# A Fourier mixing layer and a tanh-shrink MLP on one core: one third of batch 1's first stage in the prologue, half of batch 0's first matrix made on chip, other places for copies and loads

## The chip, the cores and the metric

The kernel runs on one core of a Trainium2 chip. A core has a matrix engine (PE, which loads its stationary operand in a step of its own, PEld), a vector engine (DVE), an activation engine (ACT), a general engine (POOL) and a queue engine (SP), which work at the same time and wait for each other by semaphores. Transfers between DRAM and on-chip memory run on 16 DMA engines; SP, ACT and POOL issue them, each on a queue of its own. An engine takes its instructions strictly in the order in which the program gives them, so a transfer that has to wait holds up all that its engine would do next. The metric is the device time of one execution in microseconds (us); less is better.

## The reference

```python
x = randn(8, 3008, 256) * 0.1          # batch, sequence, channels
X = rfft(x, axis=1)                    # 1505 frequencies
Y = X * (filt_r + 1j * filt_i)
y = irfft(Y, n=3008, axis=1)           # as float32
x = y.reshape(24064, 256)
h = x @ w_in                           # 256 x 2048, float64 on input
g = h - tanh(h)
out = g @ w_out                        # 2048 x 256, float64 on input
```

The outputs are 24064 x 256 float32 numbers.

## The kernel before

**The transform in four stages.** The sequence of 3008 is split as 64 x 47. With the symmetry n and 47-n, 24 residues r are left (`NH`). `first` multiplies, for each r, the 128 rows of x (64 rows for r, 64 for 47-r) by a 128 x 128 matrix `f` of cosines and sines; its 128 output rows are four blocks of 32 frequencies (`NA`): cosine and sine for each of two combinations. The result goes to DRAM (`ct1`). `middle` takes seven groups (`SLOTS`) of up to five frequencies each: `forth` mixes the 24 residues (matrices in `mats`), `filtered` multiplies by the filter, and `back` mixes back and writes to DRAM (`ct2`). `last` loads four residues at a time (`load_e2`), and its product with `g` is the input of the MLP. All products are float32.

**The MLP.** There are 48 groups of tokens (8 batches by 6), each with four quarters u of the hidden width: 192 units `U`. In unit U, `up` computes h for quarter U, the activation `shrink` works on U-1 and `down` on U-2. The first units use `up_plain` and `down_plain`, the others a scheme with 7 products in place of 8 (sums of weights, `sums`, and sums of the data, `combine`). The weights come as float64; `converted` turns a part (`raw`, 512 KB) into float32 by one ACT and six or seven DVE instructions. The eight parts of w_in are converted in the prologue, those of w_out (`late`) around its end.

**What sets the order.** The program records instructions by hand (`manual_schedule`): the order in the source is the order on each engine. Generators are stepped with `next`. In the main loop each unit has five points t(0) to t(4); the point's number in a batch is pos = 20c+5u+k, with c the group in the batch and u the quarter. `planned` spreads the 12 steps of `first` for a batch two ahead, and the 58 of `middle` for the next one, evenly over these points; while batch 0 is worked on, the steps of `first` for batch 2 have the points 2 to 34 (`LEAD`) and `middle` of batch 1 the points 34 to 104 (`LAG`). At a point, at most one due step is taken. A step of `first` issues the loads of the step two ahead (`begin`: `f` and two or three pieces of x, all by SP), two matmuls of 128 x 256, an ACT copy and a write by ACT.

**The prologue.** It does batch 0's `first` (`first0`, three parts of eight residues, with the matrices kept on chip in `f0`), then for the seven groups: `across` (transposes in place of a trip through DRAM), `forth`, `filtered`, and `back0`. Beside it stand the conversion of w_in and, in `first1`, the whole `first` of batch 1 with `f0` (12 steps of two residues; the loads `x1` in three parts, lines 222 to 228; writes at line 991). Tile `filt` has three buffers, filled from the filter inputs for group g+2 while group g is worked on (line 903); `e1`, the staging tile of the writes to `ct2`, has three. The order of transfers in the prologue is fixed by the order of issue on SP, ACT and POOL. For the later batches `filters_d` lays the filters out in DRAM (`filt_d`): it zeroes some rows from a tile `zero` (line 1072), then issues 44 copies from DRAM to DRAM by POOL (line 1081), one at each of t(1) to t(4) from unit 0 on. A function `warmer`, matmuls whose result nobody reads, is defined in the prologue and not called.

**Lines in the profile.** 867: matmuls of `first0`; 870: their copies; 888: transposes of `across`; 282 and 329: matmuls of `forth` and `back`; 298 to 310: `filtered`; 912 and 914: matmuls of `back0`; 917: its copy, 918: its write; 981: matmuls of `first1`; 250: matmuls of `first`; 426: matmuls of `last`; 534, 464: matmuls of `up_plain` and `up`; 688, 634: of `down_plain` and `down`; 141: load of a weight part; 147 to 167: its conversion; 237, 222 to 228: loads of `f` and x; 406, 408: loads for `last`.

Of the kernel before, what the change touches and what calls it, by code (L numbers as in the profile page):

```python
# [9 lines left out]
F32 = mybir.dt.float32  # L10
# [29 lines left out]

TURN, BEND, SCALE = 0.5677082594873644, 0.9282206731669795, 1.0956273529524616
NEAR = 0.6

def _consts():
# [11 lines left out]
    for r in range(NH):  # L56
        for half, n in ((0, r), (1, NR - r)):
# [5 lines left out]
            if r:  # L63
                f[half, :, r, 2, :-1], f[half, :, r, 3, :-1] = -odd * s, odd * c
            plus, minus = (1 + sign(n)) / 2, (1 - sign(n)) / 2
            f[half, :, r, 0, -1], f[half, :, r, 2, -1] = plus, minus
            if r:
                f[half, :, r, 1, -1], f[half, :, r, 3, -1] = odd * plus, odd * minus
# [14 lines left out]
    for k, (a, b) in enumerate(((cos, cos), (cos, -sin), (sin, cos), (-sin, -sin),  # L83
# [4 lines left out]

    return [np.ascontiguousarray(v, dtype=np.float32)
            for v in (f.reshape(128, -1), g.reshape(128, -1), mats, np.eye(128))]  # L90

@with_exitstack
def kernel(
# [11 lines left out]
    f_d, g_d, mats_d, one_d = (nc.inline_tensor(v, name=n).ap()  # L105
                               for v, n in zip(_consts(), ("f", "g", "mats", "one")))
# [125 lines left out]
    def first(b, z):  # L232

        def begin(c):
            w = XH * 128
            f = tr.tile([128, XH, 128], F32, tag="f", bufs=3, name="f")
            nc.sync.dma_start(f, f_d[:, w * c:w * (c + 1)])
            return load_x(tr.tile([128, XH, DM], F32, tag="x", bufs=3, name="x_sb"),
                          b, XH * c, XH), f

        began = {0: begin(0), 1: begin(1)}
        yield
        for c in range(NX):
            if c + 2 < NX:
                began[c + 2] = begin(c + 2)
            xt, f = began.pop(c)
# [27 lines left out]
    def forth(g, at, z):  # L274
# [4 lines left out]
        for v in (1, 0):  # L279
            pa = z("pa", [128, 2, DM])[0:n]  # L280
            for k in range(2):
                nc.tensor.matmul(pa[:, k], way[2 * v + k], at[0:n, 2 * v + k],  # L282
                                 start=True, stop=True)
# [548 lines left out]
    with tc.tile_pool(name="tr", bufs=2) as tr, tc.manual_schedule():  # L832
# [12 lines left out]
        with tc.tile_pool(name="pro", bufs=1) as pro, \  # L845
# [60 lines left out]
            def back0(g, nn):  # L906

                way = ways(g, 1)
                for v in range(2):
# [6 lines left out]
                    e1 = pro.tile([128, 2, DM], F32, tag="e1", bufs=3, name="e1")[0:KM]  # L916
# [11 lines left out]
            jobs = parts_of(range(4))  # L928
            xs, began = [], []
# [19 lines left out]
            G.tensor_copy(gate, xs[1][64:65, 0, 0:1])  # L949
# [6 lines left out]
            early = weights(tiles0, range(4), G, began)  # L956
# [12 lines left out]
            x1s = []  # L969

            def load_x1():

                k = len(x1s)
                x1s.append(load_x(big([128, 8, DM], F32, "x1"), 1, 8 * k, 8))

            def first1():

                for r in range(0, NH, 2):
                    pf = z0("pf", [128, 2, DM])
                    for k in range(2):  # L980
                        nc.tensor.matmul(pf[:, k], f0[:, r + k], x1s[r // 8][:, (r + k) % 8],
                                         start=True, stop=True)
                    pool, tag, bufs = ((pro, "e1", 3) if r < 12 else (tr, "a1", 2) if r < 16
                                       else (tr, "nn", 1) if r < 20 else (tr, "e1", 2))
                    if tag != "nn" or r == 16:
                        a1, n = pool.tile([128, 4 if tag == "nn" else 2, DM], F32, tag=tag,
                                          bufs=bufs, name="a1"), 0
                    ACT.copy(a1[:, n:n + 2], pf)
                    n += 2
                    if n == a1.shape[1]:  # L990
                        (ACT if r < 10 else nc.sync).dma_start(
                            dram(ct1[1], (r + 2 - n) * DM, [[NH * DM, 128], [1, n * DM]]), a1)
                    yield

            ones_1 = first1()
# [21 lines left out]
            for g in range(last_g + 1):  # L1017
# [3 lines left out]
                if g < 3:  # L1021
                    load_x1()
# [15 lines left out]
                if g in (2, 4):  # L1038
                    next(ones_1)
                if g == last_g - 1:  # L1040
# [3 lines left out]
                    fs = first(2, z1)  # L1044
                    next(fs)
            for _ in range(3):
# [3 lines left out]
            for _ in ones_1:  # L1050
                convert(5)
            convert(100)

        with tc.tile_pool(name="dn", bufs=2) as dn, \
# [15 lines left out]
            def filters_d():  # L1070
                zero = tr.tile([128, 2 * DM], F32, tag="a2", bufs=2, name="zero")
# [3 lines left out]
                                                        [1, 2 * DM]]), zero[0:n * SG])  # L1075
                nc.sync.dma_start(dram(filt_d, (n * KM * 4 + 2) * DM, [[4 * DM, 1], [1, 2 * DM]]),
                                  zero[0:1])
                yield
                for g in range(len(SLOTS)):
                    for v, row, n, src in filter_rows(g):  # L1080
                        G.dma_start(dram(filt_d, ((g * KM + row) * 4 + v) * DM,
                                         [[4 * DM, n], [1, DM]]), src)
# [144 lines left out]
```

## Time and profile before

| | |
|---|---|
| median of 3 runs | 2764.23 us |
| lowest, highest | 2760.06, 2765.8 us |
| the profiled execution's own time | 2762.34 us |
| its span, first to last instruction | 2760.5 us |
| PE busy | 2695.6 us |
| DVE, ACT, POOL busy | 1671.0, 1731.5, 1315.9 us |
| mean DMA rate over the span | 75 GB/s |

The profile is of one execution. Busy time counts work, not waiting. Of PE's time two things are not in the busy share: the waits, and how fast it ran, which is the granted clock (PEclk, 1.00 is full). A view by windows gives for each stretch of time the busy time of PE, PEld, DVE, ACT and POOL (in brackets the number of instructions), the granted clock, the mean busy share of the 16 DMA engines and their rate. In the timeline a row is: start, duration of the row's instructions together, engine, line, operation, tiles, count, and in square brackets how long the engine was idle before and what ended it. In the trace a matmul of float32 operands stands as two records (x4 is two matmuls); "SPq" and "ACTq" mark transfers being issued, and their duration is that of the issue.

### The profile page before, as it was taken

How to read it: one execution, taken by the hardware profiler on the slowest of the kernel's cores; microseconds unless marked ns; L12 is line 12 of the kernel's file. 1: busy time of each engine (PE TensorE's matmuls, PEld its weight loads, DVE VectorE, ACT ScalarE, POOL GpSimd, SP SyncE). 2: the span in 40 equal slices, each digit the busy share in tenths (PEclk: the TensorE clock that was granted, in tenths of full speed). 3: DMA queues.
4: the chain of work that ended last, by engine and by line, in shares of the span. 5: the costliest groups of instructions: out<-in, count | busy, mean ns of one | idle time of the engine just before them, and what ended most of it. 6: DMA issues, size and time to landing. Idle time of an engine off the chain costs nothing.

```text
span 2760.5 us, 36254 instructions
## 1 busy us (share of the span) xinstructions
PE 2695.6 (98%) x12866; PEld 2355.3 (85%) x12866; DVE 1671.0 (61%) x2067; ACT 1731.5 (63%) x2595; POOL 1315.9 (48%) x1106
## 2 busy tenths in 40 slices
PE   6899999999999999999999999999999999999998
PEld 5568889888898888988889888898888988899887
DVE  5776766566566665566646665466655766654545
ACT  2466666666666666666666666666666666666665
POOL 3216545454455445544545454445444554454453
PEclk9999999999999999999999999999999999999999
DMA  9743322342233312333124232332322222111010
GB/s 218 247 118 87 83 63 68 78 103 57 63 73 103 89 40 65 89 91 82 48 63 116 66 79 52 85 89 67 83 51 70 53 63 54 30 25 32 21 26 17
DMA packets 334359, 207.50 MB, mean 75 GB/s; under 512 B 226622, under 2 KB 295642, under 8 KB 333785
## 3 DMA queue, kind: packets, MB, share of 16 engines
q1 hardware_dynamic: 291529, 148.31, 23.2%
q10 hardware_dynamic: 38336, 47.72, 5.7%
q0 software_dynamic: 4304, 9.07, 1.3%
q8 instruction: 103, 1.69, 0.3%
q14 instruction: 87, 0.71, 0.1%
HBM read 133.05 MB, written 74.97 MB: 75 GB/s over the span
## 4 chain that ended last, share of the span: by engine, by line
PE 90%; DVE 4%; DMA 3%; issue 2%; ACT 1%; ACTq 0%; POOL 0%; SPq 0%; DVEq 0%; POOLq 0%
PE o L634 38%; PE x L464 22%; PE z L464 11%; PE y L464 5%; PE pa L282 3%; PE pu L426 3%; PE pe L329 3%; PE pf L250 2%; PE o L688 1%; DMA filt<-in_filt_r_dram 1%; DMA ct<-e 1%; DVE h L586 1%; DMA x<-in_x_dram 1%; DVE h L520 1%; DVE h L487 1%
## 5 line engine op out<-in xcount | busy, mean ns | idle before, releaser
L634 PE MATMUL o<-t,wd 128*128 128x256 f32 (+1 forms) x3008 | 760.3, 375 | 0.0
L444 POOL TENSOR_TENSOR t<-h 128x512 f32<-128x512 f32 (+1 forms) x186 | 256.6, 1380 | 922.9 <-DVE h L586 899.7
L586 DVE TENSOR_TENSOR h<-h,y 128x1024 f32<-128x1024 f32 (+1 forms) x384 | 512.8, 1335 | 281.5 <-ACT y L582 280.9
L634 PEld LDWEIGHTS o<-t,wd 128*128 128x128 f32 x3008 | 570.5, 190 | 69.6 <-issue 2.4
L464 PE MATMUL x<-tu,wu 128*128 128x256 f32 (+1 forms) x2256 | 574.0, 377 | 0.5 <-ACT u L470 0.2
L634 PE MATMUL o<-h,wd 128*128 128x256 f32 (+1 forms) x2256 | 571.0, 376 | 1.8 <-DVE h L586 1.8
L464 PEld LDWEIGHTS x<-tu,wu 128*128 128x128 f32 x2256 | 421.9, 190 | 61.6 <-ACT u L470 7.8
L634 PEld LDWEIGHTS o<-h,wd 128*128 128x128 f32 x2256 | 424.2, 190 | 52.7 <-DVE h L586 2.6
L470 ACT COPY s<-x 128x512 f32<-128x512 f32 (+1 forms) x188 | 108.8, 579 | 502.4 <-PE x L464 491.1
L576 ACT ACTIVATE y<-h 128x1024 f32<-128x1024 f32 (+1 forms) x384 | 400.2, 1042 | 12.5 <-ACT a L251 5.6
L579 ACT ACTIVATE y<-y 128x1024 f32<-128x1024 f32 (+1 forms) x384 | 399.6, 1040 | 12.1
L582 ACT ACTIVATE y<-y 128x1024 f32<-128x1024 f32 (+1 forms) x384 | 400.0, 1042 | 4.7
L504 DVE TENSOR_TENSOR h<-z,u 128x512 f32<-128x512 f32 (+1 forms) x188 | 127.5, 678 | 259.1 <-ACT u L470 257.8
L470 ACT COPY u<-x 128x512 f32<-128x512 f32 (+1 forms) x376 | 215.0, 572 | 85.7 <-PE x L464 65.0
L446 POOL TENSOR_TENSOR t<-h 128x512 f32<-128x512 f32 (+1 forms) x186 | 267.0, 1435 | 0.0
L445 POOL TENSOR_TENSOR t<-h,t 128x512 f32<-128x512 f32 (+1 forms) x186 | 259.8, 1397 | 14.6
L447 POOL TENSOR_TENSOR t<-h,t 128x512 f32<-128x512 f32 (+1 forms) x186 | 263.6, 1417 | 0.0
L512 DVE COPY h<-x 128x512 f32<-128x512 f32 (+1 forms) x188 | 127.9, 680 | 157.1 <-PE x L464 156.3
L464 PE MATMUL z<-ut,wu 128*128 128x256 f32 (+1 forms) x752 | 190.3, 375 | 0.0
L464 PE MATMUL z<-tu,wu 128*128 128x256 f32 (+1 forms) x752 | 190.1, 375 | 0.0
L464 PE MATMUL x<-ut,wu 128*128 128x256 f32 (+1 forms) x752 | 190.1, 375 | 0.0
L464 PE MATMUL y<-ut,wu 128*128 128x256 f32 (+1 forms) x752 | 190.0, 375 | 0.0
(137 smaller groups left out, 3085.0 us busy)
## 6 DMA issues: line engine op xcount, KB each, us to landing
e<-ct SPq DMA_DIRECT2D x48, 512.0 KB, 4.3
ct<-e ACTq DMA_DIRECT2D x96, 240.0 KB, 2.5
a<-ct SPq DMA_DIRECT2D x42, 480.0 KB, 6.9
ft<-filt SPq DMA_DIRECT2D x42, 480.0 KB, 7.5
out_dram<-ot SPq DMA_DIRECT2D x1248, 16.0 KB, 1.5
ct<-a ACTq DMA_DIRECT2D x77, 256.0 KB, 3.2
x_sb<-in_x_dram SPq DMA_DIRECT2D x138, 128.0 KB, 4.2
gt<-g SPq DMA_DIRECT2D x48, 256.0 KB, 3.2
```

The source lines that it names most:

```text
L444: by.tensor_sub(t[0], b[0][1], b[0][0])
L445: by.tensor_sub(t[1], b[1][1], t[0])
L446: by.tensor_sub(t[2], b[1][1], b[0][1])
L447: by.tensor_sub(t[3], b[1][0], t[1])
L464: nc.tensor.matmul(bank[:, k], wu[:, q - 1, (2 * u + k) * 128:(2 * u + k + 1) * 128], rhs[q - 1], start=(first and k == 0), stop=True, ski ...
L470: ACT.copy(t, X)
L512: V.tensor_copy(h[:, 2, :, 0:w], X)
L576: ACT.activation(y[k], ht[k], AF.Arctan, scale=TURN)
L579: ACT.activation(y[k], y[k], AF.Tanh, scale=BEND)
L582: ACT.activation(y[k], y[k], AF.Square, scale=SCALE, accum_out=y_sums[:, 2 * U + k // 2:2 * U + k // 2 + 1])
L586: V.tensor_mul(ht[k], ht[k], y[k])
L634: nc.tensor.matmul(product(q), wd[:, q - 1, (2 * u + k) * 128: (2 * u + k + 1) * 128], rhs[q - 1][:, k], start=(u == 0 and k == 0 and q == ...
```

## The change

There are five parts.

1. **Half of the first matrix on chip.** The four blocks of `f` are put in another order (`ORDER`, 0, 2, 3, 1), and `_consts` also returns `f_half`, the first two blocks of each residue. In this order the second half is the first one times +1 or -1, by the half of the partitions (`sgn`), but for two columns that are exchanged. The prologue loads `f_half` by ACT (three transfers of 256 KB in place of 512 KB) into tiles `fh`, and DVE makes `f0` from each with one copy and three multiplications by `sgn`, two of them of a single column per residue. `forth` takes its inputs by `PLACE`.
2. **A third of batch 1's first stage.** `first1` does eight residues (4 steps) in place of 24; one load of `x1`, issued at group 3. The other 8 steps of two residues are put ahead of batch 2's 12 in the generator `first` (`also`), which then has 20 steps at the points 4 to 34, and loads `f` and x for them from DRAM.
3. **Order of the loads at the start.** The first two weight parts are issued ahead of the third part of x, by ACT and SP; the third by POOL ahead of the filters of group 0; the fourth later, since `raw` has three buffers in place of four. `e1` has five in place of three.
4. **Matmuls for the clock.** `warmer` is called four times: 13 times on a tile of ones at the start, 5 and 8 between the parts of `first0`, 10 after the last step of `first1`.
5. **Filter copies by SP.** The 44 copies from DRAM to DRAM are issued by SP in place of POOL, from unit 2 on in place of unit 0; the tile `zero` is taken from `e1`'s buffers in place of `a2`'s.

```diff
+ORDER = (0, 2, 3, 1)
+PLACE = [ORDER.index(j) for j in range(4)]
...
+    f = f[:, :, :, ORDER, :]
     return [np.ascontiguousarray(v, dtype=np.float32)
-            for v in (f.reshape(128, -1), g.reshape(128, -1), mats, np.eye(128))]
+            for v in (f.reshape(128, -1), f[:, :, :, 0:2].reshape(128, -1), g.reshape(128, -1), mats, np.eye(128))]
...
-    def first(b, z):
-
-        def begin(c):
+    def first(b, z, also=()):
+
+        jobs = [*also, *((b, c) for c in range(NX))]
+
+        def begin(k):
+            b, c = jobs[k]
...
-                nc.tensor.matmul(pa[:, k], way[2 * v + k], at[0:n, 2 * v + k],
+                nc.tensor.matmul(pa[:, k], way[2 * v + k], at[0:n, PLACE[2 * v + k]],
...
-            def warmer(n):
-
-                warm = z0("warm", [128, 2, 128])
+            def warmer(n, t=None):
+
+                warm = z0("warm", [128, 256])
+                t = f0[:, 0:2].rearrange("p a n -> p (a n)") if t is None else t
                 for _ in range(n):
-                    nc.tensor.matmul(warm, f0[:, 0], f0[:, 0:2], start=True, stop=True)
+                    nc.tensor.matmul(warm, t[:, 0:128], t, start=True, stop=True)
...
-                    e1 = pro.tile([128, 2, DM], F32, tag="e1", bufs=3, name="e1")[0:KM]
+                    e1 = pro.tile([128, 2, DM], F32, tag="e1", bufs=5, name="e1")[0:KM]
...
-                                bufs={"raw": 4, "top": 2, "low": 1}[k])
+                                bufs={"raw": 3, "top": 2, "low": 1}[k])
...
+                if c == 2:
+                    began += [begun(tiles0, job, queue=q)
+                              for job, q in zip(jobs, (ACT, nc.sync))]
                 nc.sync.dma_start(xt[0:64], dram(x.tensor, r * DM, [[NR * DM, 64], [1, 8 * DM]]))
-                ACT.dma_start(f0[:, r:r + 8], f_d[:, 128 * r:128 * r + 1024])
+                fh = pro.tile([128, 8, 64], F32, tag="e1", bufs=5, name="fh")
+                ACT.dma_start(fh, half_d[:, 64 * r:64 * r + 512])
...
-                if lo:
-                    began += [begun(tiles0, job, queue=q)
-                              for job, q in zip(jobs, (nc.sync, ACT))]
+                V.tensor_copy(f0[:, r:r + 8, 0:64], fh)
+                for to, cols in ((64, slice(0, 64)), (95, slice(63, 64)), (127, slice(31, 32))):
+                    n = cols.stop - cols.start
+                    V.tensor_scalar(out=f0[:, r:r + 8, to:to + n], in0=fh[:, :, cols],
+                                    scalar1=sgn, scalar2=None, op0=ALU.mult)
...
+            began.append(begun(tiles0, jobs[2], queue=G))
             fts = {0: filters_of(0)}
             G.dma_start(mats[:, 3 * KM:], mats_d[:, 3 * KM:])
-            began += [begun(tiles0, job, queue=G) for job in jobs[2:4]]
...
-            convert(7)
+            warmer(13, filt[2][:, 0])
             first0(0)
+            warmer(5)
             convert(7)
             first0(1)
+            warmer(8)
+            convert(7)
             first0(2)
...
-                for r in range(0, NH, 2):
+                for r in range(0, 8, 2):
...
-                if g < 3:
-                    load_x1()
+                if g == 3:
+                    ones_1 = first1(load_x(big([128, 8, DM], F32, "x1"), 1, 0, 8))
...
-                if g in (2, 4):
-                    next(ones_1)
...
-                    fs = first(2, z1)
+                    fs = first(2, z1, [(1, c) for c in range(4, NX)])
...
-            for _ in range(3):
+            for _ in range(2):
                 next(ones_1)
             way_back()
             e2s[0] = load_e2(*groups[0])
             for _ in ones_1:
                 convert(5)
+            warmer(10)
             convert(100)
...
-                zero = tr.tile([128, 2 * DM], F32, tag="a2", bufs=2, name="zero")
+                zero = tr.tile([128, 2, DM], F32, tag="e1", bufs=2, name="zero")
...
-                        G.dma_start(dram(filt_d, ((g * KM + row) * 4 + v) * DM,
-                                         [[4 * DM, n], [1, DM]]), src)
+                        nc.sync.dma_start(dram(filt_d, ((g * KM + row) * 4 + v) * DM,
+                                               [[4 * DM, n], [1, DM]]), src)
...
-                f = [spread(NX, *((2, LEAD) if b == 2 else (0.2, LAG)), firsts, b, first)
+                f = [spread(*((NX + 8, 4, LEAD) if b == 2 else (NX, 0.2, LAG)), firsts, b, first)
...
-                    if k:
+                    if k and U > 1:
                         next(copies, None)
```

More of the change, by code (lines that the diff above doesn't have):

```diff
@@ L104 @@
     V, G, ACT = nc.vector, nc.gpsimd, nc.scalar
-    f_d, g_d, mats_d, one_d = (nc.inline_tensor(v, name=n).ap()
-                               for v, n in zip(_consts(), ("f", "g", "mats", "one")))
+    f_d, half_d, g_d, mats_d, one_d = (nc.inline_tensor(v, name=n).ap()
+                               for v, n in zip(_consts(), ("f", "f_half", "g", "mats", "one")))
     ct1 = [nc.dram_tensor(f"ct1_{b}", (4 * NA * NH, DM), F32, kind="Internal")
@@ L239, in begin @@
                           b, XH * c, XH), f
-        began = {0: begin(0), 1: begin(1)}
+        began = [begin(0), begin(1)]
         yield
[L243 to L246, printed above, removed]
+        for k, (b, c) in enumerate(jobs):
+            if k + 2 < len(jobs):
+                began.append(begin(k + 2))
+            xt, f = began.pop(0)
             pf = z("pf", [128, XH, DM])
@@ L928 @@
             jobs = parts_of(range(4))
+            sgn = cst.tile([128, 1], F32, name="sgn")
+            for half in range(2):
+                V.memset(sgn[64 * half:64 * half + 64], 1.0 - 2 * half)
+            V.memset(filt[2][:, 0], 1.0)
             xs, began = [], []
```

36 lines of the change are left out of this document (12 added, 24 removed).

## The prediction

> **What bounds the kernel now.** I read the page, then the waits of PE, then a view by windows of the first 165 us, then the transfers.
>
> ```profile
> span 2760.5 us, 36254 instructions
> PE 2695.6 (98%) x12866; PEld 2355.3 (85%) x12866; DVE 1671.0 (61%) x2067; ACT 1731.5 (63%) x2595; POOL 1315.9 (48%) x1106
> ...
> PE pf L867 <- DMA x<-in_x_dram: 17.7, 3, 8.6
> PE pf L250 <- DMA x_sb<-in_x_dram: 5.9, 1, 5.9
> PE pe L912 <- ACT e L917: 4.8, 2, 2.5
> PE pa L282 <- DVE xy L288: 4.8, 2, 4.4
> PE pu L426 <- issue: 3.0, 1, 3.0
> ```
>
> PE works 2695.6 of 2760.5 us, so a matmul moved into the main loop is paid for in full there, and what can be won are waits (total, times, longest in the rows). Those listed fall ahead of 130 us, where the change is made. To them comes PE running slowly. Columns below: length, busy PE, PEld, DVE, ACT, POOL, granted clock, DMA share, GB/s.
>
> ```profile
> 17.70:23.50 5.80, 0.00 (x1) 0.00 (x0) 3.58 (x7) 3.77 (x6) 4.22 (x8) 0.92 1.03 242
> 23.50:33.80 10.30, 10.18 (x64) 10.02 (x64) 3.96 (x8) 4.79 (x6) 5.05 (x8) 0.71 1.05 241
> 107.85:111.20 3.35, 3.35 (x16) 3.35 (x17) 1.50 (x3) 0.53 (x1) 0.00 (x0) 0.51 1.00 393
> 123.70:129.70 6.00, 0.13 (x1) 0.00 (x0) 4.35 (x8) 4.30 (x8) 6.00 (x12) 0.89 0.72 184
> 129.70:140.00 10.30, 10.26 (x24) 5.90 (x25) 3.15 (x6) 3.23 (x5) 6.26 (x11) 0.73 1.04 345
> ...
> DMA packets 11953, 21.01 MB, mean 229 GB/s; under 512 B 1529, under 2 KB 7872, under 8 KB 11564
> ```
>
> Three windows after a wait of PE show a clock of 0.71, 0.51 and 0.73. The last row is the transfers up to 91.84 us, the start of the last group's filter product: 21.01 MB at 229 GB/s, with the DMA engines full nearly throughout. The prologue is bound by transfers first.
>
> **Part 1, half of the matrix on chip, with the order of the loads.** The last two thirds of `first0` and what follows:
>
> ```profile
> 17.95 0.18 POOL L949 COPY gate<-x 1x1 f32<-1x1 f32 x1 [12.94 <-DMA x<-in_x_dram]
> 18.07 1.76 POOL L903 DMA_DIRECT2D filt<-in_filt_r_dram  x3
> 19.75 0.43 DVE L149 TENSOR_SCALAR top<-top 128x512 f32<-128x512 f32 x1 [18.48 <-ACT top L147]
> 23.54 10.18 PE L867 MATMUL pf<-f,x 128*128 128x128 f32 x64 [5.84 <-DMA x<-in_x_dram]
> 34.65 1.06 PE L888 MATMUL pq<-one_sb,wd 128*120 128x128 f32 x8 [0.93 <-ACT wd L870]
> 39.56 1.23 DVE L298 TENSOR_TENSOR nn<-xy,filt 120x1024 f32<-120x1024 f32 x1
> ```
>
> Loads shrink by 3 x 256 KB, 0.79 MB, which at 242 GB/s are 3.2 us. The second x now stands ahead of a weight part on SP; POOL's half of it was there at 17.95, so 23.54 can become about 18 to 19. All that stands in the queues up to the last x (3.15 MB of x, 1.57 of `f`, 1.05 of weight parts, 0.23 of constants: 6.0 MB before, 5.2 after) is there at 5.2 / 0.242 + 2 = 24 (2 for the start). At full clock the 64 records take 10.18 x 0.71 = 7.2 us. New on DVE: per part one copy and one multiplication of 512 elements (0.43 each, the row at 19.75) and two small ones, about 1.1 us, 3.3 in all; DVE idles 18.48 us before 19.75, which covers the first two. The third waits for the last `fh`, and delays the conversions, which stand behind it on DVE and ahead of DVE's two copies of `first0`, by up to 1 us. SP and ACT issue the same two weight parts in other places. `first0` then ends about 28.5 instead of 33.7. Against it: `forth` now needs the second copied half of `across` first (one DVE copy, 0.5 us), and the filters of group 0 stand behind a 512 KB part on POOL's queue: 0.52 MB at a third to a half of 242 GB/s is 4.3 to 6.5 us later, landing about 31 to 36 where 34 to 35 is wanted. Bounds for the filter product at 39.56: -7 to 0; I take **-4**.
>
> **Part 3, the groups.** The start of the filter product of groups 2, 4 and 6 (that of group 0 is the row at 39.56 above), ACT's longest wait, and two pieces of the chain that ended last (start, length):
>
> ```profile
> 54.16 1.23 DVE L298 TENSOR_TENSOR nn<-xy,filt 120x1024 f32<-120x1024 f32 x1
> 76.91 1.23 DVE L298 TENSOR_TENSOR nn<-xy,filt 120x1024 f32<-120x1024 f32 x1
> 91.84 1.22 DVE L298 TENSOR_TENSOR nn<-xy,filt 48x1024 f32<-48x1024 f32 x1
> ...
> 48.04 12.59 DMA filt<-in_filt_r_dram
> 60.70 8.75 DMA ct<-e
> 61.34 0.59 ACT L917 COPY e<-pe 120x512 f32<-120x512 f32 x1 [14.30 <-DMA filt<-in_filt_r_dram]
> ```
>
> Two groups take 14.6, 22.75 and 14.9 us. The first and last pair are DVE's pace; the middle pair loses 8.0 us because filters and the write of `ct<-e` stand in full queues, and ACT, with three `e1` buffers, waits 14.30 us. The change takes two of the three `x1` loads away (2.1 MB) and the 0.79 MB: 18.1 MB at 229 GB/s are there after 79 us, 12.8 before 91.84. Five `e1` buffers let ACT run 2.5 groups ahead of a write instead of 1.5. Three `raw` buffers: a part is wanted about every 13 us (seven steps, four per group of 7.3) and lands in about 10 (below), with two ahead; 0. Bounds -8.0 and 0; **-6**.
>
> ```profile
> raw<-in_moe_w_in_dram POOLq DMA_DIRECT2D x6, 512.0 KB, 9.9
> ```
>
> **Parts 2 and 4, from the last group to `last`.**
>
> ```profile
> 98.49 6.31 PE L981 MATMUL pf<-x,f 128*128 128x256 f32 x28
> 107.85 3.59 PE L426 MATMUL pu<-gt,e 128*128 128x128 f32 x16 [3.05 <-issue]
> 168.44 0.86 PE pf L250 x4
> ```
>
> Between 98.49 and 107.85 PE waits for the trip of the last `ct` write and the load of `e`, and 28 matmul records (6.31 us) lie beside it. The change leaves four matmuls and ten warmers, 14 x 0.43 = 6.0 us: hidden as before; were the trip shorter than that, they would cost the difference, 2 at most. Fewer ACT copies and `ct` writes stand beside the trip. The clock of 0.51 costs 1.7 of the 3.35 us. Bounds -3 to +1; **-1.5**. The 13 warmers at the start end, even at half clock, at 13 x 0.86 + 2 = 13 us, about when the first complete x is there today (waits of 8.6 and 17.7 - 8.6 - 5.84 = 3.3 us, a matmul between); the 5 and 8 (2.2 and 3.4 us) lie in the waits for the next x, up to 1.5 us of the 8 being in the way (inside part 1's bounds).
>
> Moved: 16 matmuls of 128x256. A step of two is 0.86 us (row at 168.44, from the chain): 8 x 0.86 = **+6.9**, with nothing to hide them as PE waits for nothing.
>
> **Loads of the moved steps.** The wait of 5.9 us at the third step in the main loop:
>
> ```profile
> 115.56 0.38 SPq L141 DMA_DIRECT2D raw<-in_moe_w_out_dram  x1
> 119.05 0.38 SPq L141 DMA_DIRECT2D raw<-in_moe_w_out_dram  x1
> 122.70 0.54 POOL zero L1072
> 123.26 0.84 SPq L1074 DMA_DIRECT2D filt<-zero  x1
> 125.02 0.52 SPq L222 DMA_DIRECT2D x_sb<-in_x_dram  x1
> 129.74 2.04 PE L250 MATMUL pf<-x_sb,f 128*128 128x256 f32 x4 [5.91 <-DMA x_sb<-in_x_dram]
> ...
> L251 ACT COPY a<-pf 128x512 f32<-128x512 f32 x7 | 4.1, 585 | 4.5 <-PE pf L250 4.5
> ```
>
> SP holds the x loads behind two weight parts, whose buffers DVE frees, and behind `zero`, which waits for such a buffer: 123.26 could be 119.5. In the new order `zero` and the copies come later and from another buffer, so the third step's x goes out 4 to 5 us earlier relative to the DVE chain, the third step itself being due at about the same place; that step would wait 0 to 2 us. But steps come every 1.5 points instead of 2.7, and the fourth stands behind a further weight part: another 1 to 3. Today's loss is 5.9 plus the low clock after it, 10.26 x 0.27 = 2.8: 8.7 us. Bounds: all gone (-8.7), or a second such wait (+8.7); nearest is the row of today's wait with SP's 3.7 us taken off: **-4**. ACT gets eight more copies of 0.59 us (last row) and their issues; it comes nearest to being full in units 1 and 2, inside these bounds.
>
> **Part 5, copies by SP.**
>
> ```profile
> L1081 POOL DMA_DIRECT2D filt<-in_filt_r_dram x22: 522/604/667, 123.2 to 257.8; - x22
> 61.39 2.35 SPq L903 DMA_DIRECT2D filt<-in_filt_r_dram  x3
> x_sb<-in_x_dram SPq DMA_DIRECT2D x16, 128.0 KB, 4.8
> ```
>
> POOL is freed of 44 x 0.6 us, and nobody waits for it there: 0. On SP such an issue takes 2.35 / 3 = 0.8 us. What queues behind it are the loads of the steps: three issues, 1.6 us, per step. A unit of 28 matmuls of 0.43 us has five points, 2.4 us each; per point SP is asked for 1.6 / 1.5 + 0.8 x 0.8 = 1.7 us. A load goes out when the step three before it has run (1.5 x 3 x 2.4 = 11 us ahead) and lands in 4.8. So **0**; without that lead it would be 0.8 us for each of some 20 copies, 16 us. The Trainium skill ("DMA: Bandwidth & Descriptors", Queues, rings and completion order) says that each DMA engine takes the issuers' queue rows in turn; the copies then lose their own row and stand in the row of the loads, which speaks against the change. No run here shows it; by it the copies cost as much as the lead lacks, today nothing.
>
> Sum: -4 - 6 - 1.5 + 6.9 - 4 = **-8.6 us**: span 2751.9, the execution 2762.34 - 8.6 = 2753.7; the median shown is 1.9 above that execution, so I say **2754**.
>
> **The rivals.**
> *Both waits go whole.* -4 - 8 - 2.5 + 6.9 - 8.7 = -16.3: 2748. For it: the 18.1 MB at 229 GB/s. Against it: the weight parts on SP remain.
> *The gain is eaten.* DVE or the filters behind the weight part set the groups' pace and little is won: -3 - 2 - 0.5 + 6.9 - 4 = -2.6: 2762. For it: `across` to the filter product is compute latency already, and DVE has 3.3 us more.
> *Slower: SP becomes the bound of units 1 to 8.* The steps' loads, weight parts, copies and `e` all stand in SP's one order. It decides from the point where the lead falls under 4.8 us plus the 1.6 and 0.8 of issue; two waits like today's on top of it make -4 - 6 - 1.5 + 6.9 + 17.4 = +12.8: 2777; one, with half of the groups' gain, -4 - 3 - 1.5 + 6.9 + 8.7 = +7.1: 2771.
> *The clock.* If the warmers end over 3 us ahead of the work, PE is slow as today: `first0` 3 us later, -5.6: 2759. The rows give waits of 5.84 and 3.05 us ahead of clocks of 0.71 and 0.51. The Trainium skill ("TensorE: Matmul & The Clock Gate", Part 1) puts the limit at an idle window of about 3.4 us; the trace agrees as far as the 5.84 us wait goes, and 3.05 is under it.
>
> **The numbers.** Forecast 0.42, whole gain 0.18, clock 0.10, eaten 0.18, slower 0.12. 2754 is the forecast's; the range 2745 to 2768 leaves out half of the slower case and the far end of the whole gain. 0.2% is 5.5 us, about what a measurement of this kernel can tell. Forecast and whole gain are faster but for their edges, the clock case lies at the bound: faster 0.63, within 0.22, slower 0.15.
>
> **What would show it.** Right: first transposes (34.65) at 29 to 31; last filter product (91.84) at 80 to 85; `last` (107.85) at 94 to 98; less than 5 us of waits of PE on `x_sb`; PE busy more by the warmers, 36 x 0.43 = 15.5 us and some. Wrong: long waits of SP on weight parts or copies with PE waiting on `x_sb`; a first filter product later than 38; PE waiting for ACT in units 1 and 2.

## The result, and the profile after

The changed kernel takes 2758.09 us (median, 2754.54 to 2760.52); the kernel before, run beside it, 2763.61 us (2760.06 to 2766.79). The ratio is 0.9981, with a 95% interval of 0.9973 to 0.9990: 5.5 us less. The two profiled executions differ by 2.9 us (2762.34 and 2759.41), but the last store goes out 4.8 us earlier (2753.47 and 2748.70); the rest is how long the last stores took, 7.0 and 8.7 us to the end of the span. The account below goes by the 4.8; both are single executions.

The page of the kernel after:

```profile
span 2757.4 us, 36442 instructions
PE 2711.3 (98%) x12938; PEld 2367.4 (86%) x12938; DVE 1676.0 (61%) x2082; ACT 1732.1 (63%) x2595; POOL 1292.4 (47%) x1062
```

PE is busy 15.7 us more and the span is shorter: what was won are waits. The waits of PE after (total, times, longest), those ahead of 130 us:

```profile
PE pe L920 <- POOL nn L312: 5.0, 4, 1.5
PE pf L255 <- DMA x_sb<-in_x_dram: 4.0, 1, 4.0
PE pf L872 <- DMA x<-in_x_dram: 2.9, 1, 2.9
PE pe L334 <- DVE xy L314: 2.0, 1, 2.0
```

The 17.7 us of waits for x in `first0` are 2.9, partly because warmers fill them; the wait of `last` (3.0) is gone; that on `x_sb` is 4.0 where it was 5.9. The timeline of PE after, at the places that the prediction named (line 872 is `first0`, 894 the transposes, 993 `first1`, 882 the warmers, 431 `last`, 255 the steps of `first`):

```profile
12.84 5.24 PE L872 MATMUL pf<-f,x 128*128 128x128 f32 x30 [2.88 <-DMA x<-in_x_dram]
31.77 1.06 PE L894 MATMUL pq<-one_sb,wd 128*120 128x128 f32 x8 [0.93 <-ACT wd L875]
...
86.98 2.36 PE L334 MATMUL pe<-xy,mats_sb 48*48 48x256 f32 x8 [2.01 <-DVE xy L314]
89.26 3.78 PE L993 MATMUL pf<-x,f 128*128 128x256 f32 x8
92.84 5.60 PE L882 MATMUL warm<-f 128*128 128x256 f32 x20
98.54 1.97 PE L431 MATMUL pu<-gt,e 128*128 128x128 f32 x16
116.88 2.04 PE L255 MATMUL pf<-x_sb,f 128*128 128x256 f32 x4 [3.98 <-DMA x_sb<-in_x_dram]
```

and the first and last filter product on DVE:

```profile
37.22 1.23 DVE L303 TENSOR_TENSOR nn<-xy,filt 120x1024 f32<-120x1024 f32 x1
82.14 1.22 DVE L303 TENSOR_TENSOR nn<-xy,filt 48x1024 f32<-48x1024 f32 x1
```

The account, place by place, in us (a minus is earlier than before):

| stretch | before | after | predicted | measured |
|---|---|---|---|---|
| to the first filter product | 39.56 | 37.22 | -4 | -2.3 |
| first to last filter product | 52.28 | 44.92 | -6 | -7.4 |
| last filter product to the end of `last` | 19.60 | 18.37 | -1.5 | -1.2 |
| moved matmuls | | | +6.9 | +6.9 (taken over) |
| loads of the moved steps | | | -4 | -0.8 |
| sum | | | -8.6 | -4.8 |

The moved matmuls were not measured apart: 8 x 0.86 is taken over from the prediction, and the loads' term is the remainder. `last` ends 10.9 us earlier (111.44 and 100.51), the first product of `down` comes 5.7 us earlier (193.48 and 187.80), and by then 18 steps have run in place of 11, 7 x 0.86 = 6.0 us. The last two of the 20 steps bring the other 0.9.

### The profile page after: what moved, and what is told of

Read it like the earlier page. It is cut to its first block, busy times and chain, and to the rows that moved or that the text cites. A ratio compares the mean times of both kernels' runs of the same rounds, so it can differ in the third digit from the quotient of the medians.

```text
span 2757.4 us, 36442 instructions
## 1 busy us (share of the span) xinstructions
PE 2711.3 (98%) x12938; PEld 2367.4 (86%) x12938; DVE 1676.0 (61%) x2082; ACT 1732.1 (63%) x2595; POOL 1292.4 (47%) x1062
## 4 chain that ended last, share of the span: by engine, by line
PE 91%; DVE 5%; issue 2%; DMA 1%; ACT 1%; ACTq 0%; SPq 0%; POOL 0%; DVEq 0%; POOLq 0%
PE o L639 38%; PE x L469 22%; PE z L469 11%; PE y L469 5%; PE pa L287 3%; PE pe L334 3%; PE pu L431 3%; PE pf L255 2%; PE o L693 1%; DVE h L591 1%; DVE h L525 1%; DVE h L492 1%; DVE xy L324 0%; PE pf L872 0%; PE o L539 0%
```

## The experiments

Two questions were open: whether moving two thirds of batch 1's first stage (8 of its 12 steps) into the main loop pays; and why the groups became 7.4 us faster. The reasons predicted for the groups were fewer `x1` loads and five `e1` buffers. "Groups" is the time from the first to the last filter product.

**The moved steps: undone, and given a longer lead.** `e_all_first` puts all 12 steps of batch 1 back into the prologue, with their three `x1` loads, and has no warmers behind them.

```diff
-                for r in range(0, 8, 2):
+                for r in range(0, NH, 2):
...
-                if g == 3:
-                    ones_1 = first1(load_x(big([128, 8, DM], F32, "x1"), 1, 0, 8))
+                if g < 3:
+                    load_x1()
...
-                    fs = first(2, z1, [(1, c) for c in range(4, NX)])
+                    fs = first(2, z1)
...
-            warmer(10)
```

> Part 2 of the change undone, without the ten last warmers: the whole first stage of batch 1 in the prologue again, the other parts kept (half matrix on chip, order of the loads, five e1 buffers, three raw buffers, first warmers, copies by SP). Theory (2.1 MB of x more keep the queues full and the groups lose part of what they won, the main loop has 6.9 us of matmuls less): last filter product at 85 to 90 us instead of 82.1, the time within 4 us of the changed kernel, on either side. Rival 1 (five e1 buffers alone made the groups fast): groups as fast as in the changed kernel, the time 4 to 7 us below it. Rival 2 (the smaller load alone made them fast): last filter product back at 89 or later and the time 2 us or more above the changed kernel.

It takes 2750.28 us, ratio 0.9956 (0.9942 to 0.9969), and its groups 44.9 us; DVE and PE in its timeline:

```profile
38.25 1.23 DVE L303 TENSOR_TENSOR nn<-xy,filt 120x1024 f32<-120x1024 f32 x1
83.18 1.22 DVE L303 TENSOR_TENSOR nn<-xy,filt 48x1024 f32<-48x1024 f32 x1
99.25 1.97 PE L431 MATMUL pu<-gt,e 128*128 128x128 f32 x16 [1.43 <-ACT a L1007]
```

Moving the two thirds thus costs some 7 us (0.9981 - 0.9956, of 2763; the two intervals do not overlap). In the prologue the 16 matmuls delay hardly anything: `last` starts at 99.25 with them and at 98.54 without. From there to the last store (2737.48) this kernel needs 11.9 us less than the changed one. If 6.9 of that are the matmuls, 5.0 are left for the wait for `x_sb` and the clock after it (its own such wait is 1.65 us). And the 2.1 MB of `x1` do not slow the groups: the first reason is wrong.

`e_three_ahead` keeps the moved steps, but issues a step's loads three steps ahead in place of two, so that the third step's go out in the prologue:

```diff
-        began = [begin(0), begin(1)]
+        began = [begin(0), begin(1), begin(2)]
...
-            if k + 2 < len(jobs):
-                began.append(begin(k + 2))
...
+            if k + 3 < len(jobs):
+                began.append(begin(k + 3))
```

> The generator of the first stage begins three loads ahead instead of two: the third step's f and x are issued in the prologue, ahead of the weight parts on SP, and the later ones right after the matmuls of the step that frees the buffer. Theory (SP's order, the two weight parts whose buffers DVE frees, makes PE wait 3.98 us on x_sb at the third step and then run at a clock of 0.66 over 8.1 us): the wait goes and with it the slow stretch, 4.0 + 8.1 x 0.34 = 6.7 us at most, 4 to 7 us less than the changed kernel. Rival (the loads are late because the DMA engines are full at that time, share 1.08): the wait moves to the fourth step and the time changes by less than 1.5 us.

2754.40 us, ratio 0.9972 (0.9960 to 0.9984). PE no longer waits for `x_sb`; in its timeline two small waits for ACT take the place:

```profile
96.63 1.97 PE L431 MATMUL pu<-gt,e 128*128 128x128 f32 x16
99.57 1.77 PE L539 MATMUL x<-ut,wu 128*128 128x448 f32 x4 [0.96 <-ACT ut L434]
115.45 1.13 PE L253 MATMUL pf<-x_sb,f 128*128 128x256 f32 x4 [1.00 <-ACT a L254]
```

From `last` (96.63) to the last store (2742.28) it needs 4.5 us less than the changed kernel; 3.98 of wait and 8.10 x 0.34 = 2.8 of clock (the window at 116.90, below), less these two, would be 4.8. The intervals of the two kernels overlap, but the trace shows that the wait on the loads was real. Why the change did not take it away, SP's timeline of the kernel after shows:

```profile
105.57 0.42 SPq L413 DMA_DIRECT2D e<-ct  x1
108.14 0.38 SPq L143 DMA_DIRECT2D raw<-in_moe_w_out_dram  x1
108.56 0.47 SPq L242 DMA_DIRECT2D f<-f  x1
109.61 0.63 SPq L230 DMA_DIRECT2D x_sb<-in_x_dram  x1
```

The third step's loads still stand behind a weight part, which DVE releases at 108.1; and right behind its 512 KB the last piece takes 7.1 us to land (109.6 to 116.75), where the same load took 4.0 in the kernel before (both rows are shown below).

**The groups: buffers, bytes, order.** `e_three_e1` takes the `e1` tiles (`e1`, `a1`, `fh`) back from five buffers to three.

```diff
...
-                fh = pro.tile([128, 8, 64], F32, tag="e1", bufs=5, name="fh")
+                fh = pro.tile([128, 8, 64], F32, tag="e1", bufs=3, name="fh")
...
```

> Three e1 buffers as before the change, all else as changed. Theory (the smaller load and the five buffers share the groups' gain of 7.4 us): ACT waits for a write of ct again, groups 1 to 4 us slower. Rival (the smaller load alone made it): groups within 1 us, no difference in the time.

2756.95 us, ratio 0.9979 (0.9970 to 0.9988); groups 44.9 us (38.57 to 83.48). The second reason is wrong too. Taken away together, `e_all_first_three_e1` has the edits of both:

> The whole first stage of batch 1 in the prologue again and three e1 buffers, the rest as changed (half matrix, order of the loads, three raw buffers, warmers but the last ten, copies by SP). So far the groups took 45 us from the first to the last filter product with either of the two alone. Theory (either of them is enough: fewer loads or more buffers): with neither the groups are slow again, 49 to 53 us, and the time is 3 to 8 us above that of the kernel with five buffers. Rival (the third thing, the smaller first load and the weight parts issued later, made the groups fast): 45 to 46 us, no difference to five buffers.

2750.32 us, ratio 0.9948 (0.9933 to 0.9964); groups 44.9 us again. A third thing makes the groups fast. Its counterpart `e_before_five_e1` is the kernel before with the five `e1` and three `raw` buffers alone (the fourth weight part goes out later for it):

```diff
-                    e1 = pro.tile([128, 2, DM], F32, tag="e1", bufs=3, name="e1")[0:KM]
+                    e1 = pro.tile([128, 2, DM], F32, tag="e1", bufs=5, name="e1")[0:KM]
...
-            began += [begun(tiles0, job, queue=G) for job in jobs[2:4]]
+            began += [begun(tiles0, job, queue=G) for job in jobs[2:3]]
```

> The kernel before with five e1 buffers; to make room for them raw has three buffers and the fourth weight part is issued when the first has been converted, after the filters of groups 0 and 1. Theory (buffers are enough, even with the whole x and f): groups 45 to 47 us instead of 52.3, the time 4 to 7 us below the kernel before. Rival (before the change the filters themselves came late through full queues): groups 49 us or more, time within 2 us of before.

2763.87 us, ratio 0.9998 (0.9989 to 1.0007); groups 54.9 us. ACT, in its timeline, stands as in the kernel before:

```profile
48.34 0.57 ACT L917 COPY e<-pe 120x512 f32<-120x512 f32 x1
63.09 0.60 ACTq L918 DMA_DIRECT2D ct<-e  x1
63.73 0.59 ACT L917 COPY e<-pe 120x512 f32<-120x512 f32 x1 [14.83 <-DMA filt<-in_filt_r_dram]
```

So no buffer was missing. It is the write that stands, not the copy, and it is released by a load of filters, with which it shares no data. In ACT's timeline of the kernel before:

```profile
46.46 0.59 ACT L917 COPY e<-pe 120x512 f32<-120x512 f32 x1 [0.45 <-PE pe L914]
60.70 0.60 ACTq L918 DMA_DIRECT2D ct<-e  x1
```

and in ACT's timeline of the kernel after:

```profile
43.61 0.59 ACT L923 COPY e<-pe 120x512 f32<-120x512 f32 x1 [0.45 <-PE pe L920]
44.23 0.60 ACTq L924 DMA_DIRECT2D ct<-e  x1
45.34 0.59 ACT L923 COPY e<-pe 120x512 f32<-120x512 f32 x1 [1.14 <-PE pe L920]
```

The waits in the built program (not a profile) tell why. A transfer signals its landing by a semaphore. The transfers of SP and ACT take eight of them (`DMAHW0` to `DMAHW7`) in turn, and each waits first until the transfer that held its semaphore before has landed. Of the kernel before, the load of group 4's filters on SP and the first write on ACT, and the write of the kernel after with the load that held its semaphore (the number is the transfer's place among those of its engine):

```
before SP   24  L903 DMACopy filt_75<-in_filt_r_dram  [waits DMAHW3_49,DMASW4_49,DVE_49]
before ACT   5  L918 DMACopy ct_0<-e_348              [waits DMAHW3_49,Activation_49]
after  SP   15  L909 DMACopy filt_74<-in_filt_r_dram  [waits DMAHW2_49,DMASW6_49]
after  ACT   5  L924 DMACopy ct_0<-e_387              [waits DMAHW2_49,Activation_49]
```

Before, the write has the turn after load 24, which goes out only when DVE has done with the buffer (48.04) and lands at 60.63: the row of 12.59 us in the chain that the prediction shows, and the write at 60.70 the next row. The third write on ACT has the turn after the first, which takes 8.75 us to land, and goes out at 69.53. After, the first write's turn is after load 15, issued by 40.9. The built programs of all fourteen kernels agree: in the three whose groups take 52.3, 52.6 and 54.9 us the first write has the turn after load 24, and in the eleven whose groups take 44.9 us after load 15, 16 or 18, all of group 3's filters. Which turn a transfer gets is dealt out when the program is built; it can't be read from the source, and instructions put ahead of the write on other engines move it. The next two runs differ in nothing else: one has more matmuls on PE, and the fill of the tile that they read.

`e_before_part_order` is the kernel before with the weight parts in the new order (and three `raw` buffers):

```diff
+                if c == 2:
+                    began += [begun(tiles0, job, queue=q)
+                              for job, q in zip(jobs, (ACT, nc.sync))]
...
+            began.append(begun(tiles0, jobs[2], queue=G))
             fts = {0: filters_of(0)}
```

> The kernel before, with the weight parts ordered as in the changed kernel (first two ahead of the third x by ACT and SP, third by POOL ahead of the filters of group 0, three raw buffers); no half matrix, no warmers, three e1, all of batch 1 in the prologue. What is to be told apart: what made the seven groups fast. Theory, the turn of the semaphores: in the built program each transfer issued by SP or ACT takes one of eight semaphores in turn, and its issue waits until the transfer that held it before has landed. In the kernel before, ACT's first write of e holds the semaphore of the load of group 4's filters, which goes out at 48.04 and lands at 60.63; ACT stands from 47.05 to 60.70. In this kernel the turn is the same, so ACT's first write should go out at 58 to 64, some 13 us or more after its copy, the time from the first to the last filter product should be 51 to 56 us, and the whole 2760 to 2766 (ratio 0.9985 to 1.001). Rival, the order of the weight parts: the filters of groups 1 to 3 meet emptier queues; then 45 to 47 us from first to last, no ACT wait above 4 us, and a ratio near 0.997.

2760.58 us, ratio 0.9993 (0.9983 to 1.0002). Groups 52.6 us; DVE and ACT in its timeline:

```profile
37.48 1.23 DVE L298 TENSOR_TENSOR nn<-xy,filt 120x1024 f32<-120x1024 f32 x1
...
46.53 0.57 ACT L917 COPY e<-pe 120x512 f32<-120x512 f32 x1
57.68 0.60 ACTq L918 DMA_DIRECT2D ct<-e  x1
58.32 0.59 ACT L917 COPY e<-pe 120x512 f32<-120x512 f32 x1 [11.22 <-DMA filt<-in_filt_r_dram]
...
90.12 1.22 DVE L298 TENSOR_TENSOR nn<-xy,filt 48x1024 f32<-48x1024 f32 x1
```

`e_before_part_order_warm` adds the warmers of 13, 5 and 8, whose results nobody reads, and fills the tile that the 13 read:

```diff
+            warmer(13, filt[2][:, 0])
             first0(0)
+            warmer(5)
...
+            warmer(8)
             first0(2)
```

> The same kernel as e_before_part_order with one thing more: warmers of 13, 5 and 8 matmuls in the prologue, as in the changed kernel. The order of the instructions on SP, ACT and POOL is the same in both. They move, in the order in which the building of the program deals out the semaphores, ACT's first write ahead of the load of group 4's filters. Theory, the turn of the semaphores: ACT's first write goes out within 3 us of its copy, at 44 to 49, first to last filter product 44.5 to 47 us, and the whole is 7 to 11 us shorter than e_before_part_order: 2752 to 2757, ratio 0.9958 to 0.9977. Rival, the warmers do no more than raise the clock in first0: the first filter product comes 1 to 3 us earlier, the groups take as long as in e_before_part_order (51 to 56), and the whole is 1 to 3 us shorter than that kernel.

2756.64 us, ratio 0.9979 (0.9969 to 0.9988), 3.9 us less than its twin; nine of its ten times lie below the lowest of the twin's ten (2757.80). Groups 44.9 us, in the same view:

```profile
39.86 1.23 DVE L298 TENSOR_TENSOR nn<-xy,filt 120x1024 f32<-120x1024 f32 x1
...
46.93 0.56 ACT L918 COPY e<-pe 120x512 f32<-120x512 f32 x1
47.52 0.60 ACTq L919 DMA_DIRECT2D ct<-e  x1
...
84.79 1.22 DVE L298 TENSOR_TENSOR nn<-xy,filt 48x1024 f32<-48x1024 f32 x1
```

The copy stands at the same time in both (46.53 and 46.93); the write goes out 10.2 us earlier, and the groups are 7.7 us shorter. The turn of the semaphores holds; the whole gained less than expected, since in this pair the first filter product came 2.4 us later and `last` took 3.17 us at a low clock in place of 1.97. Which part of the change brings the write its good turn there is not shown: the turn is good with the warmers and all `x1` loads (`e_all_first`) and with no warmers and a third of the `x1` loads (`e_no_warmers`, below), but both keep the half matrix. Not tried was the write with another turn and nothing else changed. Nor was the bad turn behind a load that lands soon: the 12.59 us of that load, with the DMA engines full (share 1.07 from 40 to 60 us), set how long the write stood.

**The start.** `e_full_matrix` loads the whole of `f` by ACT, in the new order of columns:

```diff
-                ACT.dma_start(fh, half_d[:, 64 * r:64 * r + 512])
+                ACT.dma_start(f0[:, r:r + 8], f_d[:, 128 * r:128 * r + 1024])
...
-                V.tensor_copy(f0[:, r:r + 8, 0:64], fh)
```

> The first matrix is loaded whole again (three times 512 KB), without the DVE instructions that make its second half; all else as changed. Theory (the load of 0.79 MB is worth what it takes, 3.2 us at 242 GB/s): first transposes at 34 to 35 us instead of 31.8, the time 2 to 3 us above the changed kernel. Rival (the first x, complete at 12.8 us, the matmuls and the warmers between the parts set the pace, and the order of the loads made the gain): transposes within 1 us of 31.8, no difference in the time.

2759.22 us, ratio 0.9986 (0.9977 to 0.9995), its interval overlapping that of the changed kernel. In the trace it is plainer: transposes at 34.30 in place of 31.77, first filter product at 41.27, groups 44.9. With the warmers in place the half matrix is thus worth 2.5 us at the transposes. Without them it shows less: the new order of the parts alone brings the transposes from 34.65 to 32.57 (`e_before_part_order`; first filter product at 37.48), and the kernel with the half matrix and no warmers (`e_no_warmers`, below) has them at 31.78. The order with warmers and the whole matrix has them at 34.96 (first filter product at 39.86).

**The clock.** `e_no_last_warmers` leaves out the ten after `first1`, `e_no_warmers` all four calls:

```diff
-            warmer(10)
```

> The ten warmers after the first stage of batch 1 left out, all else as changed. Theory (they run until 98.44 us, and the product of last starts at 98.54 with no wait: they stand in its way, the load of e having been issued at 91.94): last starts 1 to 2.5 us earlier but at half clock (3.6 instead of 2.0 us), so the time is within 1.5 us. Rival (e lands only about 98): the start stays, the slow clock costs 1.6 us more.

> All four calls of the warmers left out, all else as changed. Theory (in the first part the work waits for x, so warmers cost nothing and a clock near full saves 1.4 us on each of two parts, less the 8 that stand between): first transposes 0 to 3 us later than 31.8, the time 0 to 3 us above the changed kernel. Rival (the 5 and 8 stand in the way of data that are there): transposes 1 to 3 us earlier, the time 1 to 3 us below.

2759.01 us, 0.9985 (0.9976 to 0.9994), and 2760.01 us, 0.9992 (0.9983 to 1.0001); groups 44.9 us in both (39.92 to 84.82 and 39.48 to 84.39). In both `last` waits and runs slow; in the second 3.64 us after a wait of 3.2, in the first, by PE's timeline:

```profile
98.74 3.64 PE L431 MATMUL pu<-gt,e 128*128 128x128 f32 x16 [5.27 <-issue]
```

The trip from the last filter product to `last` is then 13.9 us (84.82 to 98.74), where the kernel after has 16.4 (82.14 to 98.54, without a wait): the ten warmers, at low clock 5.60 us, run past the arrival of `e` by an estimated 2.5 us and save 1.7 in `last`. In `e_three_e1`, where they take 4.48 us, PE still waits 1.05 us for `e` behind them, and the trip is 14.0 us. Their worth is within what these runs can tell. All warmers together are worth 2.5 us by the medians (5.5 and 3.0 us below the kernel before), and the two intervals overlap.

**The copies.** `e_copies_by_pool` gives the 44 filter copies back to POOL:

```diff
-                        nc.sync.dma_start(dram(filt_d, ((g * KM + row) * 4 + v) * DM,
+                        G.dma_start(dram(filt_d, ((g * KM + row) * 4 + v) * DM,
```

> The 44 filter copies issued by POOL again, from unit 2 on as in the changed kernel. Theory (SP has time for them, and the wait at the third step comes ahead of the first copy): no difference, within 1 us. Rival (the copies on SP delay the loads of the steps): PE waits less on x_sb, the wait of 0.8 us at 166.4 goes, the time 1 to 4 us below the changed kernel.

2755.85 us, ratio 0.9975 (0.9966 to 0.9984): not to be told from the changed kernel (the intervals overlap). In both, PE waits for `x_sb` ahead of 119 us only, and the changed kernel's first copy goes out at 130.8.

**Both kernels beaten.** `e_all_first_three_ahead` has the edits of `e_all_first` and `e_three_ahead`:

> The whole first stage of batch 1 in the prologue, without the last ten warmers, and loads of the first stage three steps ahead. Theory (what the two do apart adds up, the second as far as the wait of 1.6 us and a slow clock after it go): 0 to 3 us below the kernel with the whole first stage alone, 2748 to 2750. Rival (a third load in the prologue delays the load of e): last starts later by 1 us or more, and the time is not below it.

2746.51 us, ratio 0.9936 (0.9923 to 0.9950): 17 us less than before, three times what the change brings.

## Why the prediction was right, and where not

The total was inside the range and the sign was right; 2754 was predicted, 2758 measured. By its steps:

- *Part 1, -4 predicted, -2.3 measured.* The transposes came at 31.77, behind the 29 to 31 said, the first filter product at 37.22. The half matrix was worth up to 2.5 us (`e_full_matrix`) of the 3.2 that its bytes say. What was mis-sized is DVE's work, put at "up to 1 us", and the free place given to the warmers. In the kernel after, 10 and 16 records of warmers stand between the parts of `first0`, which ends at 30.8 in place of 28.5. Without them it ends at 27.35, and still the transposes start at 31.78, after a wait of 4.42 us: DVE makes the last third of `f0` only when its `fh` has landed (22.18), twelve instructions of conversion stand behind that, and then come DVE's two copies of `first0`, which the transposes need. DVE and PE in the timeline of `e_no_warmers`:

```profile
22.18 0.43 DVE L954 COPY f<-fh 128x512 f32<-128x512 f32 x1 [14.00 <-DMA fh<-f_half]
...
30.23 1.45 DVE L875 COPY wd<-pf 128x512 f32<-128x512 f32 x2
31.78 1.54 PE L894 MATMUL pq<-one_sb,wd 128*120 128x128 f32 x8 [4.42 <-issue]
```

In the kernel after, the same two copies start at 30.17, so PE's chain and DVE's end together, and taking out the warmers alone brings no earlier transposes. What the warmers saved lies behind the transposes: in the kernel after PE waits 0.93 us there and the first filter product follows 5.5 us later; behind the wait of 4.42 it follows 7.7 us later (39.48), with the first eight records of `forth` in 3.77 us in place of 1.99, and behind one of 3.07 (`e_no_last_warmers`) 8.0. `forth` waits 0.78 us for the copied half, about the 0.5 said. Profiled executions whose start is built alike show the first filter product at 36.97, 37.22, 38.13, 38.57 and 39.92, so a single one tells this term to within 3 us only.
- *The groups, -6 predicted, -7.4 measured: the size right, the reasons wrong.* The step that failed is "the middle pair loses 8.0 us because filters and the write of `ct<-e` stand in full queues, and ACT, with three `e1` buffers, waits 14.30 us". Neither the `x1` bytes nor the buffers did it; the write waited for the semaphore of a load. Full queues had a part in it at most by the 12.59 us that this load took to land. The quoted row named the releaser, `filt<-in_filt_r_dram`, at ACT's next copy; for a missing buffer one would expect `ct<-e` there. That the size came out was luck: the two reasons that gave it are wrong.
- *The tail, -1.5 predicted, -1.2 measured.* The clock of `last` came out as said (1.97 us), and the bound "they would cost the difference, 2 at most" is about what the warmers cost.
- *Moved matmuls, +6.9.* `e_all_first` shows the loss in the whole, some 7 us with its loads. The prediction had this price right and did not draw what follows from it: the second of the five parts is a loss. PE busy rose by 15.7 where 15.5 were said for the warmers, but by luck: the warmers were busy 19.8 us, since some ran at a low clock, and all else on PE 4.1 us less.
- *Loads, -4 predicted, -0.8 measured.* This mis-sized term is most of the miss. The load of the third step did go out 5.0 us earlier, counted from the end of `last` (14.1 us behind it before, 9.1 after), and the step was due at the same place (12.4 us behind it in both). But "today's wait with SP's 3.7 us taken off" leaves the landing as it was, and that grew from 4.02 to 7.14 us, with the last piece going out 1.5 us behind 512 KB (the chain that ended last, before and after):

```profile
125.58 4.02 DMA x_sb<-in_x_dram
...
109.61 7.14 DMA x_sb<-in_x_dram
```

So PE waited 3.98 us, and the clock after it was as low as before (0.66 over 8.1 us, 0.73 over 10.3). Why the load took longer was not tried apart. A wait for ACT cost another 0.8 us, once (the kernel after, in a view by windows with the columns as in the prediction, and PE's timeline):

```profile
116.90:125.00 8.10, 8.10 (x19) 5.14 (x20) 3.24 (x7) 2.59 (x5) 0.00 (x0) 0.66 0.87 254
```

```profile
166.36 1.13 PE L469 MATMUL x<-tu,wu 128*128 128x256 f32 x4 [0.82 <-ACT u L475]
```

- *Copies by SP, 0 predicted.* No wait of PE on `x_sb` follows the first copy. The Trainium skill ("DMA: Bandwidth & Descriptors", Queues, rings and completion order) has each DMA engine take the issuers' queue rows in turn; by the prediction's reading the copies would then cost what the lead of the loads lacks. The lead lacks nothing once they go out, so the runs speak neither for the rule nor against it.
- *The rivals.* Waits of SP on weight parts with PE waiting on `x_sb`, named as a sign against the forecast, did show, once. So did what speaks for the gain being eaten, DVE's work ahead of the transposes.

## What to carry to other kernels

Where an engine waits at a transfer that it issues, read the releaser's name before giving the wait a reason: a transfer can stand behind another with which it shares neither data nor buffer, only a semaphore, and then more buffers do not help. When such turns are dealt out at build time, an edit elsewhere can shift them, here by 7.7 us of the groups and 3.9 of the whole; compare the semaphores of the two built programs along with the order. A stage moved into a loop that is full pays its whole work there. A load that is moved among other neighbours does not keep its time to land: the same one took 4.0 and 7.1 us here. Where taking work out brings nothing, look for another engine whose work ends at the same time.

## What was not expected of the hardware

PE ran slow after waits much shorter than the 5.84 and 3.05 us of the prediction. In the changed kernel a wait of 2.01 us at 86.98 is followed by eight records of `first1` in 3.78 us (the granted clock from 89.3 to 92.8 is 0.50); `e_three_ahead`, `e_copies_by_pool` and `e_no_warmers` have the same wait (2.00 to 2.01) and take 3.68, 3.55 and 3.78. In `e_three_e1`, `e_full_matrix` and `e_no_last_warmers` the wait there is 0.32 to 0.45 us, and the same eight records take 1.99 to 2.00. The Trainium skill ("TensorE: Matmul & The Clock Gate", Part 1) puts the limit at an idle window of about 3.4 us; here 2.0 us were enough, four times of four, and the measurement decides. The timeline of `e_three_e1`, for comparison with the rows of the kernel after above:

```profile
88.32 1.90 PE L334 MATMUL pe<-xy,mats_sb 48*48 48x256 f32 x8 [0.32 <-DVE xy L314]
90.14 2.00 PE L993 MATMUL pf<-x,f 128*128 128x256 f32 x8
```

The length of one wait does not decide it, though. In the kernel after, waits of 0.36 and 1.30 us end at 69.89 and 71.86, and the granted clock from 71.9 to 78.0 is 0.50. In `e_three_e1` waits of the same two lengths end at 71.24 and 73.20, and the clock from 73.2 to 79.0 is 1.00. What else decides stays open (PE's timelines, the kernel after first):

```profile
71.86 1.21 PE L920 MATMUL pe<-nn,mats_sb 120*120 120x256 f32 x2 [1.30 <-POOL nn L312]
72.86 1.06 PE L918 MATMUL pe<-nn,mats_sb 120*120 120x256 f32 x2
...
73.20 0.69 PE L920 MATMUL pe<-nn,mats_sb 120*120 120x256 f32 x2 [1.30 <-POOL nn L312]
73.73 0.59 PE L918 MATMUL pe<-nn,mats_sb 120*120 120x256 f32 x2
```
